# Sliding-window attention and a spectral mixing layer on one core: when the weights are prefetched, and into which slots

## The chip, the cores and the metric

The kernel runs on one core of a Trainium2 chip. The metric is the device time of one execution in microseconds (us). Ten runs of the kernel before took 462.46 to 473.84 us, with a median of 468.85 us.

The core has TensorE (PE, matmuls; PEld is its weight load), VectorE (DVE), ScalarE (ACT), GpSimd (POOL) and SyncE (SP). Here SP issues the plain DMA transfers, and POOL issues those that cast from fp32 to bf16 on the way. In the profile, q1 is SP's queue and q0 is POOL's.

## What is computed

The inputs are q, k and v of shape (8, 8, 576, 64) (batch, heads, sequence, head size), 64 pairs of weight matrices `w_r[m]`, `w_i[m]` of 512 x 512, and one matrix `w_ch` of 512 x 512, all fp32.

```python
# attention: window of 128 keys, a slope per head
scores = q @ k.T / sqrt(64) - slope[h] * |i - j|      # only 0 <= i - j < 128
x = softmax(scores) @ v                               # heads side by side: (8, 576, 512)

# spectral mixing
X = rfft(x, axis=1)                                   # the first 64 modes are used
Yr[b, m] = Xr[b, m] @ w_r[m] - Xi[b, m] @ w_i[m]
Yi[b, m] = Xr[b, m] @ w_i[m] + Xi[b, m] @ w_r[m]
u = x + irfft(Y, n=576, axis=1)                       # the other modes are zero
out = u + relu(u @ w_ch)                              # (8, 576, 512) fp32
```

Nearly all of the bytes are the 128 weight matrices. Each is 1 MB (1024 KB), and is used once, for all eight batches together.

## The kernel before, in words

**Attention.** The work is cut into 16 units. A unit is one batch element and four heads. A software pipeline runs over stages, and `STAGE` lists what is done in a stage, in the order in which each engine gets it, with a lag: an entry with lag -2 works on the unit that is two ahead. DVE casts the loaded fp32 q, k and v to bf16 (`cast`, L225), PE transposes q and k, ACT or DVE copies the result out of PSUM, PE makes the scores, ACT takes exp, DVE multiplies by a mask or PE adds a bias, PE multiplies by v, and DVE normalises into `x` (`norm`, L347). After every second unit the batch element is complete, and PE makes its 64 modes by a matmul with the table `F`; they are stored in `XC`.

The raw q, k and v lie in two slots each. `cast` of unit u ends with `load` of unit u + 2 into the slot that it has just read, so a load is issued only when DVE gets to that cast. Casts of q run three stages ahead, of k two ahead and of v in the unit's own stage. The last k load is therefore issued in stage 11, and the last v load in stage 13.

**The setup.** `_forward_table` (L71) makes `F` by a Sin on ACT, and then POOL puts the last rows of the table in place (L100 to L102). `distances` (L141) makes on POOL the two tables `near`, from which the masks (`decay`, ACT) and the biases (`offset`, DVE) of the heads are made. `fixtures` (L128) sets constant parts of the two v buffers and of the two `att` buffers on POOL. The masks and biases of heads 4 to 7 are made beside the first stages, from the list `side`.

**Weight tiles.** A weight tile is one matrix, numbered 0 to 127 in the order of use, `w_r[0]`, `w_i[0]`, `w_r[1]` and so on. `load_w` (L440) loads the next tiles in one of two forms. As bf16 a tile takes half the space and is issued by POOL. As fp32 it is issued by SP, and PE reads the upper halves of its numbers as bf16. Before the change tiles are loaded strictly in the order of use:

- In the attention, as bf16, into the pool `early` of `EARLY` = 14 slots: `AHEAD` gives for each stage how many. From stage 1 on a small copy (`gate`) makes POOL wait for the first `norm` of the stage before it issues them. `LATER` does the same for seven slots in the raw q, k and v buffers that are no longer needed (`spare`). Tiles 0 to 20 are loaded in this way.
- At the end of the attention, as fp32, into `NWA` = 6 slots that lie where attention buffers were: tiles 21 to 26.
- In the mixing, `AGAIN` = 12 bf16 tiles into the slots of `early` that come free (27 to 38), each issued after one of the first 12 tiles has been used; and from then on, fp32 tiles, each into the fp32 slot of the tile just used. When tile `K1` - 1 = 38 has been used, `NWB` = 2 more fp32 slots are opened, and the space is taken for `wch`, `Zs` and `XW`.

**Mixing.** For each tile PE runs four matmuls (L604). Four modes share a PSUM tile (`acc`), which DVE scales and PE transposes into `YT`. From tile `K1` on, PE also makes the product of `x` with `w_ch` between the weight matmuls (`project`, L574). After the last tile the inverse transform, relu and sum run over 36 output tiles, which SP stores.

**What sets the order.** Each engine has its instructions in program order (`manual_schedule`); there is no planner. POOL's queue holds the setup, the gates and all bf16 loads; SP's holds the q, k and v loads, then all fp32 loads, then the stores. An instruction that waits holds up all behind it in its queue.

Of the kernel before, what the change touches and what calls it, by code (L numbers as in the profile page):

```python
# [10 lines left out]
BF16 = mybir.dt.bfloat16  # L11
# [8 lines left out]
P = 128  # L20
# [6 lines left out]
FULL = 4  # L27
# [43 lines left out]
def _forward_table(nc, pool, F, S):  # L71


    NM = F.shape[2] // 2
    tok = pool.tile([P, FULL + 1], I32)
    nc.gpsimd.iota(tok[:, :FULL], [[P, FULL]], base=0, channel_multiplier=1)
    for bb in range(2):
        nc.gpsimd.iota(
            tok[64 * bb : 64 * bb + 64, FULL : FULL + 1], [[0, 1]],
            base=FULL * P, channel_multiplier=1,  # L80
        )
    mode = pool.tile([P, NM], I32)
    nc.gpsimd.iota(mode, [[1, NM]], base=0, channel_multiplier=0)
    prod = pool.tile([P, FULL + 1, NM], FP32)
    nc.vector.tensor_tensor(
        out=prod,
        in0=tok.unsqueeze(-1).broadcast_to([P, FULL + 1, NM]),
        in1=mode.unsqueeze(1).broadcast_to([P, FULL + 1, NM]),
        op=ALU.mult,
    )  # L90
    turn = pool.tile([P, FULL + 1, 2, NM], FP32)
    for ri in range(2):
        nc.vector.tensor_scalar(turn[:, :, ri, :], prod, float(S) / (4 - 2 * ri), 1.0 / S,
                                op0=ALU.add, op1=ALU.mult)
    whole = pool.tile([P, FULL + 1, 2, NM], FP32)
    nc.vector.tensor_scalar(whole, turn, MAGIC, MAGIC, op0=ALU.add, op1=ALU.subtract)
    nc.vector.tensor_tensor(out=turn, in0=turn, in1=whole, op=ALU.subtract)
    nc.scalar.activation(F[:, : FULL + 1].rearrange("p a b -> p (a b)"),
                         turn.rearrange("p a b c -> p (a b c)"), AF.Sin, scale=TWO_PI)
    nc.gpsimd.memset(F[:64, FULL + 1], 0.0)  # L100
    nc.gpsimd.tensor_copy(F[64:, FULL + 1], F[64:, FULL])
    nc.gpsimd.memset(F[64:, FULL], 0.0)  # L102


class _Attention:
# [19 lines left out]
        self.att = [fix.tile([P, FULL * 8 * P + 64], BF16, name=f"att{i}") for i in range(2)]  # L125
        self.loaded, self.casted, self.open = {}, {}, {}

    def fixtures(self):  # L128
        nc = self.nc
        for t, tail in zip(self.vb, self.vt):  # L130
            for half in range(2):
                row = slice(64 * half, 64 * half + 64)
                c0 = W * half
                nc.gpsimd.memset(t[row, :, :, :, W - c0 : 2 * W - c0], 0.0)
                nc.gpsimd.memset(t[row, :, :, :, c0 + D : c0 + W], 1.0)
            nc.gpsimd.memset(tail, 0.0)
            nc.gpsimd.memset(tail[64:96, :, :, D:], 1.0)
        for t in self.att:
            nc.gpsimd.memset(t[:, FULL * 8 * P :], 1.0)

    def distances(self, pool):  # L141

# [254 lines left out]
def kernel(  # L397
# [10 lines left out]
    nc = tc.nc  # L408
    ctx.enter_context(tc.manual_schedule(engines=ALL | {SP}))
    B, H, S, _ = q.shape  # L410
    NM, DM, _ = moe_w_r.shape
    AHEAD = {0: 1, 1: 1, 3: 1, 4: 1, 5: 1, 7: 1, 8: 1, 10: 1, 11: 1, 12: 2, 13: 2, 14: 1}
    EARLY, NWA, NWB, AGAIN = 14, 6, 2, 12
    LATER = {11: 1, 12: 2, 13: 1, 14: 1, 15: 2}
    HM = NM // 2

    const = ctx.enter_context(tc.tile_pool(name="const", bufs=1))
# [3 lines left out]
    F = const.tile([P, FULL + 2, 2 * NM], BF16, name="F")  # L421
# [5 lines left out]
    early = actx1.enter_context(  # L427
        tc.tile_pool(name="w1", bufs=EARLY, side="right", reuse_waits="tile")
    )
# [4 lines left out]
    vflat = raw["v"].rearrange("p u s h d -> p (u s h d)")  # L434
    spare += [vflat[:, 2 * DM * i :] for i in range(3)]
    spare = [t[:, : 2 * DM].bitcast(BF16).rearrange("p (a e) -> p a e", a=4) for t in spare]
    wq, homes = [], []

    def load_w(n, pool, bf16):


        for i in range(len(wq), min(len(wq) + n, 2 * NM)):
            src = (moe_w_r, moe_w_i)[i % 2][i // 2].rearrange("(p a) e -> p a e", a=4)
            homes.append(pool)
            if bf16:
                t = spare.pop(0) if pool is None else pool.tile([P, 4, DM], BF16, tag="w", name="w")
                nc.gpsimd.dma_start(out=t, in_=src)
                wq.append([t[:, a] for a in range(4)])
            else:
                t = pool.tile([P, 4, DM], FP32, tag="w", name="w")  # L450
                nc.sync.dma_start(out=t, in_=src)
                wq.append([t[:, a].bitcast(BF16)[:, 1::2] for a in range(4)])

    with ExitStack() as actx:
        at = _Attention(tc, actx, q, k, v, (ident, F, FT), x, XC, raw)
        n = len(at.units)
        for w, u in (("q", 0), ("k", 0), ("q", 1), ("k", 1), ("v", 0), ("v", 1)):
            at.load(w, u)
        done = set()

        def run(name, arg, u):
            if 0 <= u < n and (name, arg, u) not in done:
                done.add((name, arg, u))
                getattr(at, name)(u, arg)

        make_identity(nc, ident)
        pool = _Scratch(x[:, B - 2 :].rearrange("p b t c -> p (b t c)").bitcast(FP32))
        wt = at.ps.tile([P, P], FP32, tag="av", bufs=1, name="warm")
        for _ in range(24):
            nc.tensor.matmul(wt, lhsT=ident, rhs=ident, start=True, stop=True)  # L470
        _forward_table(nc, pool, F, S)
        nc.vector.memset(norm, 2.0 / S)
        nc.vector.memset(norm[:32], 1.0 / S)
        for t in at.qkT:
            nc.vector.memset(t[:, 1, :, S:], 0.0)
        at.distances(pool)
        at.fixtures()
        nc.gpsimd.memset(XC[:, 4 * NC * NM :], 0.0)
        run("cast", "q", 0)
        run("transpose", "q", 0)  # L480
        run("cast", "k", 0)
        run("transpose", "k", 0)
        run("evacuate", "q", 0)
        for h in (1, 3):
            at.decay(h)
        run("evacuate", "k", 0)
        run("score", 1, 0)
        for h in (1, 3, 0, 2):
            at.offset(h)
        run("cast", "q", 1)  # L490
        run("transpose", "q", 1)
        run("evacuate", "q", 1)
        run("score", 0, 0)
        run("exp", 1, 0)
        for h in (0, 2):
            at.decay(h)
        run("exp", 0, 0)
        run("cast", "k", 1)
        run("cast", "v", 0)
        side = {0: [(at.offset, 4), (at.offset, 5), (at.offset, 6), (at.offset, 7), (at.decay, 5),  # L500
                    (at.decay, 7)], 1: [(at.decay, 4), (at.decay, 6)]}
        lags = [lag for _, _, lag in STAGE]
        for stage in range(min(lags), n + max(lags)):
            for name, arg, lag in STAGE:
                run(name, arg, stage - lag)
                if name in ("transpose", "exp") and side.get(stage):
                    fn, h = side[stage].pop(0)
                    fn(h)
            for fn, h in side.pop(stage, ()):
                fn(h)  # L510
            if stage == 3:
                at.inverse_table()
            if stage in AHEAD:
                if stage:
                    b, g = at.units[stage - 1]
                    nc.gpsimd.tensor_copy(gate[:1, :1], x[:1, b, 0, 256 * g : 256 * g + 1])  # L516
                load_w(AHEAD[stage], early, True)
            if stage in LATER:
                load_w(LATER[stage], None, True)

    with ExitStack() as mctx:
        fix = mctx.enter_context(tc.tile_pool(name="fix", bufs=1))
        YT = fix.tile([P, 2, 4, B, 2, HM], BF16, name="YT")
        pool = mctx.enter_context(tc.tile_pool(name="fin", bufs=2))
        wpool = mctx.enter_context(tc.tile_pool(name="w", bufs=NWA, reuse_waits="tile"))
        load_w(NWA, wpool, False)
        pctx = ExitStack()
        ps = pctx.enter_context(tc.tile_pool(name="fps", bufs=2, space=PSUM))
# [60 lines left out]
        def warm():  # L589
            wt = ps.tile([P, DM], FP32, tag="warm", bufs=1, name="warm")  # L590
            for _ in range(6):
                nc.tensor.matmul(wt, lhsT=ident, rhs=wch[:, 0], start=True, stop=True)  # L592

        quads, side, todo = [], [], 0
        Zs = XW = wch = w2 = None
        K1 = EARLY + sum(LATER.values()) + NWA + AGAIN
        for g in range(NM // 4):
            acc = ps.tile([P, DM], FP32, tag="acc", bufs=2, name="acc")
            for i in range(8):
# [10 lines left out]
                    )  # L610
                k = 8 * g + i
                if k < AGAIN:
                    load_w(1, early, True)
                elif homes[k] not in (early, None):
                    load_w(1, homes[k], False)
                if k == K1 - 1:
                    actx1.close()
# [19 lines left out]
                elif 8 * g + i >= 2 * NM - 5:  # L637
                    if 8 * g + i < 2 * NM - 1:
                        warm()
                if k >= K1 and k % 2 == 0 and todo < len(tiles):  # L640
                    side.append(project(todo))
# [110 lines left out]
```

## Time and profile before

| | |
|---|---|
| runs, median | 468.85 us |
| profiled execution, time | 470.03 us |
| profiled execution, span | 468.3 us |
| PE, DVE, ACT, POOL busy | 341.1, 181.3, 159.0, 58.3 us |
| read from and written to HBM | 163.58 MB, 9.44 MB |
| first weight matmul of the mixing | 148.66 us |

The profile is of one execution. Its page cuts the span into 40 slices of 11.7 us; a digit is the busy share in tenths. The GB/s count the bytes as they land, so that a tile cast to bf16 counts half of what is read. The DMA share of a stretch adds the times of packets, which overlap a little, over 16 engines: full use shows as slightly over 1. A wait is listed as the engine and line that waited, what released it, and then microseconds in total, number of times, and the longest.

### The profile page before, as it was taken

Reading aid. Unit: us, or ns where it says so; the run is one execution under the profiler, and the core shown is the slowest. Engines: PE = TensorE matmul, PEld = TensorE weight load, DVE = VectorE, ACT = ScalarE, POOL = GpSimd, SP = SyncE. Lnnn points to the kernel's source line nnn. Section 1 sums busy time; section 2 is a strip of 40 time slices with the busy share of each in tenths; the row PEclk is TensorE's granted clock in tenths of the full one; section 3 lists DMA queues with packets and bytes.
Section 4 is the critical chain, followed back from the end, with each engine's and each line's share of the span. In section 5 each row is a group of like instructions: output and inputs, shape, how many; then the busy total and the mean of one; then the engine's idle time right before and its main releaser. Section 6 shows DMA issues by size and latency. Waiting matters only on the chain.

```text
span 468.3 us, 7360 instructions
## 1 busy us (share of the span) xinstructions
PE 341.1 (73%) x2975; PEld 188.3 (40%) x3006; DVE 181.3 (39%) x353; ACT 159.0 (34%) x211; POOL 58.3 (12%) x101
## 2 busy tenths in 40 slices
PE   3579899997296844347997767876778687598994
PEld 3357667675265511113433333333333233233331
DVE  5879699993473200001211202121111120104785
ACT  4779799997081000000111111111102011003773
POOL 5600001021121201000000000000000000000654
PEclk8679899999699966557999999899989899869998
DMA  8899999999899999997999999999999999980787
GB/s 284 252 303 336 304 264 304 308 302 232 187 205 319 328 316 316 315 297 212 422 423 421 418 423 422 418 421 421 418 423 421 419 422 421 421 371 33 242 285 250
DMA packets 52146, 155.67 MB, mean 332 GB/s; under 512 B 3984, under 2 KB 22928, under 8 KB 39952
## 3 DMA queue, kind: packets, MB, share of 16 engines
q1 hardware_dynamic: 46832, 137.38, 77.1%
q0 software_dynamic: 5280, 17.83, 19.3%
q8 instruction: 23, 0.38, 0.3%
q14 instruction: 11, 0.09, 0.1%
HBM read 163.58 MB, written 9.44 MB: 369 GB/s over the span
## 4 chain that ended last, share of the span: by engine, by line
DMA 56%; PE 20%; DVE 10%; issue 7%; ACT 4%; POOL 2%; POOLq 0%; DVEq 0%; ACTq 0%
DMA w<-in_moe_w_r_dram 40%; DMA w<-in_moe_w_i_dram 8%; PE acc L604 7%; DMA kr<-in_k_dram 5%; PE av L331 3%; DVE x L347 2%; DMA qr<-in_q_dram 2%; PE warm L592 1%; DVE vb L233 1%; DVE att L305 1%; PE tp L250 1%; ACT r L686 1%; PE my L585 1%; DVE k L238 1%; DVE o L695 1%
## 5 line engine op out<-in xcount | busy, mean ns | idle before, releaser
L604 PE MATMUL acc<-w,XC 128*32 128x512 bf16 x484 | 133.6, 430 | 69.5 <-DMA w<-in_moe_w_i_dram 34.4
L604 PEld LDWEIGHTS <-XC 128*32 128x32 bf16 x512 | 59.8, 138 | 128.2 <-issue 99.2
L587 ACT CAST XW<-my 128x512 bf16<-128x512 f32 x36 | 21.1, 586 | 219.5 <-PE my L585 143.7
L294 ACT ACTIVATE att<-sc 128x1024 bf16<-128x1024 f32 x64 | 64.2, 1031 | 9.8 <-PE sc L284 9.8
L581 DVE COPY xT<-tr 128x512 bf16<-128x512 bf16 x36 | 15.3, 425 | 116.9 <-PE tr L579 116.9
L689 POOL TENSOR_TENSOR r<-r,x 128x512 f32<-128x512 f32 x18 | 20.8, 1158 | 261.5 <-ACT r L686 261.5
L331 PE MATMUL av<-vb,att 128*128 128x132 bf16 (+1 forms) x576 | 40.3, 223 | 17.2 <-DVE x L347 15.4
L331 PEld LDWEIGHTS <-att 128*128 128x128 bf16 x704 | 38.6, 101 | 23.1 <-issue 9.9
L585 PE MATMUL my<-wch,xT 128*128 128x512 bf16 x134 | 38.1, 394 | 7.9 <-DVE xT L581 7.3
L533 DVE TENSOR_SCALAR yq<-acc 128x512 bf16<-128x512 f32 x15 | 10.3, 686 | 73.6 <-PE acc L604 73.6
L256 ACT COPY qkT<-tp 128x1152 bf16<-128x1152 bf16 x30 | 33.5, 1115 | 13.9 <-PE tp L250 13.3
L284 PE MATMUL sc<-qkT 64*64 64x256 bf16 (+2 forms) x640 | 26.2, 272 | 7.8 <-ACT qkT L256 3.9
L347 DVE TENSOR_TENSOR x<-av,rec 128x640 bf16<-128x640 f32 x32 | 26.4, 825 | 1.1
L695 DVE TENSOR_TENSOR o<-yy,r 128x512 f32<-128x512 f32 x36 | 23.7, 688 | 6.5 <-ACT r L686 4.9
L233 DVE CAST vb<-vr 64x1024 bf16<-64x1024 f32 x32 | 22.8, 711 | 6.5 <-DMA vr<-in_v_dram 6.3
L686 ACT ACTIVATE r<-mm 128x512 f32<-128x512 f32 x36 | 21.2, 597 | 9.0 <-PE mm L676 5.0
L284 PEld LDWEIGHTS <-qkT 64*64 64x64 bf16 x640 | 14.9, 111 | 22.0 <-issue 16.4
L585 PEld LDWEIGHTS <-xT 128*128 128x128 bf16 x144 | 11.4, 100 | 28.9 <-issue 11.3
L564 ACT CAST Zs<-zw 64x512 bf16<-64x512 f32 x16 | 9.2, 578 | 34.9 <-PE zw L555 34.7
L305 DVE TENSOR_TENSOR att<-att,mask 128x1024 bf16<-128x1024 bf16 x32 | 20.6, 684 | 0.0
L565 DVE CAST Zs<-z 64x512 bf16<-64x512 f32 x16 | 11.0, 688 | 18.1 <-PE z L558 18.0
L516 POOL COPY gate<-x 1x1 bf16<-1x1 bf16 x11 | 5.4, 490 | 97.9 <-DVE x L347 97.9
(93 smaller groups left out, 336.1 us busy)
## 6 DMA issues: line engine op xcount, KB each, us to landing
w<-in_moe_w_i_dram SPq DMA_DIRECT2D x48, 1024.0 KB, 18.8
w<-in_moe_w_r_dram SPq DMA_DIRECT2D x47, 1024.0 KB, 18.8
qr<-in_q_dram SPq DMA_DIRECT2D x16, 576.0 KB, 8.4
kr<-in_k_dram SPq DMA_DIRECT2D x16, 576.0 KB, 7.8
vr<-in_v_dram SPq DMA_DIRECT2D x32, 256.0 KB, 7.5
out_dram<-o SPq DMA_DIRECT2D x32, 256.0 KB, 2.5
w<-in_moe_w_r_dram POOLq DMA_DIRECT2D x13, 512.0 KB, 9.4
w<-in_moe_w_i_dram POOLq DMA_DIRECT2D x13, 512.0 KB, 9.5
```

The source lines that it names most:

```text
L233: nc.vector.tensor_copy(self.vb[u % 2][row, :, :, :, W * half : W * half + D], src[row, :2])
L256: (self.nc.vector.tensor_copy if u < 2 and w == "q" else self.nc.scalar.copy)(dst.rearrange("q h (p j) -> q h p j", j=TPP), tp.rearrange(" ...
L284: nc.tensor.matmul(sc[64 * half : 64 * half + 64, e, j * 256 + c0 : j * 256 + c0 + n], lhsT=qkT[row, 1, h, k0 + j : k0 + P : 2], rhs=qkT[r ...
L294: self.nc.scalar.activation(self.att[u % 2][:, kt * 8 * P : (kt + 1) * 8 * P], sc.rearrange("p e n -> p (e n)"), AF.Exp, scale=1.0 / math. ...
L305: nc.vector.tensor_tensor(out=rows, in0=rows, in1=self.table[:, heads], op=ALU.mult)
L331: nc.tensor.matmul(bank[:, qt * W : qt * W + rhs[j].shape[1]], lhsT=att[:, o : o + P], rhs=rhs[j], start=(n == 0 and j == 0), stop=(n == l ...
L347: nc.vector.tensor_tensor(out=self.x[:, b, :, cs].rearrange("p t (h d) -> p h t d", h=2), in0=tiles[:, :, :, :D], in1=rec.unsqueeze(-1).br ...
L585: nc.tensor.matmul(mm, lhsT=xT[:, dt], rhs=wch[:, dt], start=(dt == 0), stop=(dt == 3))
L587: nc.scalar.copy(XW[:, i], mm)
L604: nc.tensor.matmul(acc[32 * (i // 2) : 32 * (i // 2) + 32], lhsT=XC[:, c0 : c0 + 31 * NM + 1 : NM], rhs=w[a], start=(ri == 0 and a == 0), ...
L686: nc.scalar.activation(r, mm, AF.Relu)
L695: nc.vector.tensor_tensor(out=o, in0=yy, in1=r, op=ALU.add)
```

## The change

The diff changes five things.

1. `_forward_table` becomes a generator: it stops after the Sin, and POOL's last steps on `F` run between the first and the second half of the fixtures, after `distances`.
2. The biases of the first heads are made in the order 0, 2, 1, 3, and the eight side steps for heads 4 to 7 all run in stage 0, two of them at each transpose.
3. The prefetch: one tile moves from stage 3 to stage 2. The tiles of stage 12 (two in `early` and two spare) and one spare tile of stage 11 are dropped from there. Stage 13 loads four, stage 14 four, stage 15 three: 20 tiles instead of 21.
4. The transition: `load_w` can take a chosen tile, and the tiles not yet loaded are kept in a list. The eight recycled bf16 slots get tiles 24, 26, ... 38, and the fp32 slots get the numbers between in order (20 to 23, 25, 27, 29, ...).
5. `AGAIN` is 8 instead of 12; `K1` is computed from the last chosen tile and is 39 as before.

```diff
@@ _forward_table @@
     nc.scalar.activation(F[:, : FULL + 1].rearrange("p a b -> p (a b)"),
                          turn.rearrange("p a b c -> p (a b c)"), AF.Sin, scale=TWO_PI)
+    yield
     nc.gpsimd.memset(F[:64, FULL + 1], 0.0)
     nc.gpsimd.tensor_copy(F[64:, FULL + 1], F[64:, FULL])
     nc.gpsimd.memset(F[64:, FULL], 0.0)
@@ fixtures @@
-    def fixtures(self):
+    def fixtures(self, i):
         nc = self.nc
-        for t, tail in zip(self.vb, self.vt):
+        for t, tail in ((self.vb[i], self.vt[i]),):
...
-        for t in self.att:
-            nc.gpsimd.memset(t[:, FULL * 8 * P :], 1.0)
+        nc.gpsimd.memset(self.att[i][:, FULL * 8 * P :], 1.0)
@@ the kernel's function @@
-    AHEAD = {0: 1, 1: 1, 3: 1, 4: 1, 5: 1, 7: 1, 8: 1, 10: 1, 11: 1, 12: 2, 13: 2, 14: 1}
-    EARLY, NWA, NWB, AGAIN = 14, 6, 2, 12
-    LATER = {11: 1, 12: 2, 13: 1, 14: 1, 15: 2}
+    AHEAD = {0: 1, 1: 1, 2: 1, 4: 1, 5: 1, 7: 1, 8: 1, 10: 1, 11: 1, 13: 4, 14: 1}
+    LATER = {14: 3, 15: 3}
+    EARLY, NWA, NWB, AGAIN = 14, 6, 2, 8
...
-    wq, homes = [], []
+    wq, homes, todo_w, again = {}, {}, list(range(2 * NM)), []

-    def load_w(n, pool, bf16):
+    def load_w(n, pool, bf16, chosen=None):
-        for i in range(len(wq), min(len(wq) + n, 2 * NM)):
+        for i in ([i for i in todo_w if i not in again][:n] if chosen is None else chosen):
+            todo_w.remove(i)
             src = (moe_w_r, moe_w_i)[i % 2][i // 2].rearrange("(p a) e -> p a e", a=4)
-            homes.append(pool)
+            homes[i] = pool
...
-        _forward_table(nc, pool, F, S)
+        table = _forward_table(nc, pool, F, S)
+        next(table)
...
         at.distances(pool)
-        at.fixtures()
+        at.fixtures(0)
+        next(table, None)
+        at.fixtures(1)
...
-        for h in (1, 3, 0, 2):
+        for h in (0, 2, 1, 3):
             at.offset(h)
...
-        side = {0: [(at.offset, 4), (at.offset, 5), (at.offset, 6), (at.offset, 7), (at.decay, 5),
-                    (at.decay, 7)], 1: [(at.decay, 4), (at.decay, 6)]}
+        side = {0: [(at.offset, 4), (at.offset, 6), (at.decay, 5), (at.offset, 5), (at.decay, 7),
+                    (at.offset, 7), (at.decay, 4), (at.decay, 6)]}
...
                 if name in ("transpose", "exp") and side.get(stage):
-                    fn, h = side[stage].pop(0)
-                    fn(h)
-            for fn, h in side.pop(stage, ()):
-                fn(h)
+                    for _ in range(1 + (name == "transpose")):
+                        fn, h = side[stage].pop(0)
+                        fn(h)
...
         wpool = mctx.enter_context(tc.tile_pool(name="w", bufs=NWA, reuse_waits="tile"))
+        first = todo_w[0]
+        again = [first + 4 + 2 * i for i in range(AGAIN)]
         load_w(NWA, wpool, False)
...
-        K1 = EARLY + sum(LATER.values()) + NWA + AGAIN
+        K1 = again[-1] + 1
...
                 if k < AGAIN:
-                    load_w(1, early, True)
+                    load_w(1, early, True, again[k : k + 1])
```

More of the change, by code (lines that the diff above doesn't have):

```diff
@@ L447, in load_w @@
                 nc.gpsimd.dma_start(out=t, in_=src)
-                wq.append([t[:, a] for a in range(4)])
+                wq[i] = [t[:, a] for a in range(4)]
             else:
@@ L451, in load_w @@
                 nc.sync.dma_start(out=t, in_=src)
-                wq.append([t[:, a].bitcast(BF16)[:, 1::2] for a in range(4)])
+                wq[i] = [t[:, a].bitcast(BF16)[:, 1::2] for a in range(4)]
     with ExitStack() as actx:
```

## The prediction

> **What bounds the kernel now.** I read the page first: its slices over time and its DMA queues.
>
> ```profile
> span 468.3 us, 7360 instructions
> ...
> DMA  8899999999899999997999999999999999980787
> GB/s 284 252 303 336 304 264 304 308 302 232 187 205 319 328 316 316 315 297 212 422 423 421 418 423 422 418 421 421 418 423 421 419 422 421 421 371 33 242 285 250
> ...
> q1 hardware_dynamic: 46832, 137.38, 77.1%
> q0 software_dynamic: 5280, 17.83, 19.3%
> ...
> DMA 56%; PE 20%; DVE 10%; issue 7%; ACT 4%; POOL 2%; POOLq 0%; DVEq 0%; ACTq 0%
> ```
>
> The DMA engines are busy in nearly every slice up to 420 us. The low GB/s before slice 19 are partly a matter of counting: a tile that is cast to bf16 on the way is read as 1 MB and counted as the 0.5 MB that land. So 315 GB/s with half of the tiles cast is 315 x 4/3 = 420 GB/s read, the same rate as the 422 later. The DMA is therefore the bound until the last weight lands, whatever the engines do, and what can be saved is the time in which the DMA engines have nothing to do. The second view is the table of stretches, which shows where that is (stretch, its length, PE, PEld, DVE, ACT and POOL busy, clock, DMA share, GB/s). The share counts overlapping packets, so a saturated stretch shows 1.01 to 1.07.
>
> ```profile
> 2.00:16.00 14.00, 5.71 (x63) 4.11 (x61) 9.68 (x18) 6.25 (x9) 9.63 (x22) 0.70 1.07 337
> 16.00:20.00 4.00, 2.75 (x40) 1.41 (x37) 3.99 (x5) 3.31 (x4) 3.83 (x8) 0.77 0.61 200
> 20.00:100.00 80.00, 69.30 (x1250) 54.54 (x1262) 70.80 (x129) 70.84 (x81) 7.28 (x16) 0.94 1.07 299
> ...
> 112.00:124.00 12.00, 4.22 (x76) 3.39 (x75) 1.85 (x4) 3.88 (x6) 0.00 (x0) 0.84 1.07 236
> 124.00:130.00 6.00, 3.94 (x45) 3.38 (x44) 4.63 (x9) 0.74 (x1) 2.04 (x4) 0.50 0.65 124
> ...
> 200.00:212.00 12.00, 5.59 (x12) 1.55 (x12) 0.00 (x0) 0.00 (x0) 0.00 (x0) 0.50 1.05 286
> 212.00:218.50 6.50, 4.70 (x21) 1.89 (x21) 1.31 (x5) 0.00 (x0) 0.00 (x0) 0.70 0.47 88
> 218.50:418.00 199.50, 151.74 (x689) 67.14 (x701) 32.24 (x80) 25.74 (x44) 0.00 (x0) 0.95 1.01 421
> ```
>
> Three holes stand out: 16 to 20 us, 124 to 130 us and 212 to 218.5 us. Each is priced as its length times one minus its share over its neighbours' share: 4 x (1 - 0.61/1.07) = 1.7 us; 6 x (1 - 0.65/1.07) = 2.3 us; 6.5 x (1 - 0.47/1.05) = 3.6 us. Together 7.6 us. In 112 to 124 the engines stand still (DVE busy 1.85 of 12 us) and yet the DMA is full. Who is late there is told by the waits from 108 to 128 us (us in total, times, longest), and the third hole by SP's own waits:
>
> ```profile
> DVE vb L233 <- DMA vr<-in_v_dram: 6.3, 1, 6.3
> DVE k L238 <- DMA kr<-in_k_dram: 2.9, 1, 2.9
> DVE q L238 <- DMA qr<-in_q_dram: 2.0, 1, 2.0
> DVE vt L235 <- DMA vr<-in_v_dram: 1.2, 1, 1.2
> ```
>
> ```profile
> SPq L451 <- PE acc L604: 98.0, 43, 34.3
> ```
>
> The attention loses 6.3 + 2.9 + 2.0 + 1.2 = 12.4 us to its own last loads, and in the third hole SP has waited 34.3 us for PE to free an fp32 slot.
>
> **What the Trainium skill says.** "DMA: Bandwidth & Descriptors", section "Queues, rings and completion order": an engine takes turns between the queues that have work, a packet at a time. The trace agrees, and shows what that means for unequal packets. From 105 to 120 us the POOL queue q0 had 706 packets and SP's queue q1 807, nearly one to one, but q0 held 85.2% of the engines' time and q1 20.0%, because a weight row is 8 KB read and a v row 512 bytes. A k load (issued at 100.11) took 24.1 us to land. The same page, "Issuing engines are not separate DMA queues": work issued by SP and by POOL shares the same 16 engines. It agrees: with both queues running from 148 to 200 us the share is 1.04, not more. "HBM Reference", section "Access", gives about 425 GB/s for a core streaming alone; here it is 421 from 218.5 to 418 us. One 1.0486 MB tile thus costs 1.0486/0.421 = 2.49 us of DMA, and moving it in time gains nothing by itself.
>
> **The setup.** POOL waits 3.61 us for the Sin at L101, and L100 to L102 stand from 1.88 to 6.83 us, ahead of the distances. With these behind the first half of the fixtures the distances end 4.9 us sooner. Waiting on them are the bias at L176 (DVE idle 2.66 us) and the mask at L173 (ACT idle 2.31 us). Then DVE goes on right after its copy that ends at 7.95 us, and the casts after that, each of which issues the load of two units later, come up to 2.66 us sooner. So do the loads missing in the first hole. POOL's wait of 3.61 us vanishes, and its first weight load (19.37 us) comes about 3.6 us sooner, into the same hole; q, k and v loads beside it are held up as they were by it before. After 20 us the DMA is full again, so a longer lead of the compute gains nothing: the most is the 1.7 us of the hole. The least is 0; I take 1.3. The order of the biases and of the side decays (eight pieces, all in stage 0 now) moves DVE pieces of 0.66 us and ACT pieces of 0.6 us within stretches where the DMA is full: nothing; if that cover went, up to 1.3 us for two decays, two pieces of 0.6, counted in the lower end.
>
> **The weight of stage 3 in stage 2.** One load goes from 43.37 us to about 35 us. The DMA is full on both sides: 0. If it makes a q, k or v load late, the engines wait up to 2.5 us, but the DMA works on meanwhile.
>
> **The prefetch held back.** Before, POOL issues six tiles between 100.35 and 110.36 us; after, one, and nothing in stage 12. Five tiles leave the stretch: 5 x 2.49 = 12.4 us of DMA. The attention should regain about its 12.4 us, but the five tiles have to be loaded later: the two cancel. What counts is idle DMA. The hole at 124 to 130 us is there because stage 13 and its gate were late; it goes: -2.3 us. Against it, the DMA may now run dry before the held-back tiles start. Counting the trace's packets by size, 3.2 MB were asked for and not yet read at 100.35 us (about 2.1 loads of q or k, one of v, 1.3 weights). At some 385 GB/s, what I count as read from 100 to 110 us, that lasts 8.3 us, to 108.7. v of unit 14, asked for at about 105 us, adds 0.59 MB, 1.75 us at 340 GB/s: to 110.4. Unit 13's v cast (before at 118.32 after its wait) would then stand at about 110.4 to 112.2, and frees the slot for the last v load; POOL's gate opens after the next norm, two to three DVE pieces on, at about 113.6. Between 110.4 and 112.2 the DMA is idle, from then on the last v load fills it. New idle: 1.8 us; at 421 GB/s throughout it would be 3 us, with slower draining 0. Behind the gate on POOL stand only further weight loads, and who waits for these is PE, after the attention. From 113.6 us eleven bf16 tiles are 27 us of DMA; the first six fp32 loads, which wait for attention memory (139.99 to 146.7 us before), come some 12 us sooner, so no hole opens at the end of the attention.
>
> **Every second tile recycled.** Now the twelve bf16 tiles are one block, numbers 27 to 38, and 39 to 46 load at the same time into eight fp32 slots. The two queues go half and half, so all arrive near 212 us; PE waits for 38, then has to free slots before SP can issue (216.33 us). After, the eight bf16 tiles are every second number from 24 to 38, and the fp32 tiles the numbers between: what arrives together is used together, each tile used frees a slot, and SP never sits on a full pool. While q0 has tiles, it covers any short gap of q1; when it ends, q1 has up to eight slots out. The hole goes: -3.6 us; by bytes not read it is up to 4.4 us, and 0 if q1 restarts as late as now. PE has room: four matmuls take 1.05 us per tile against 2.49 us. Five more tiles come in fp32 instead of bf16: both are read at 420 GB/s, 0.
>
> **Sum.** -1.3 - 2.3 + 1.8 - 3.6 = -5.4 us. What follows the last weight (420 to 468.3 us) is unchanged. The profiled execution took 470.03 us, 1.7 us more than its span, so 464.6 for it; it lies 1.2 us above the median of 468.85, so for the median 463.4 us.
>
> **The rivals.** (1) The DMA conserves more than I think: the dry spell before the gate is 5 us, and the third hole only goes by half. -1.3 - 2.3 + 5 - 1.8 = -0.4, about 468.4 us. For it: only two v loads are asked for after 100.4 us. Against: 3.2 MB of backlog. (2) The holes are worth more: counted by bytes, the second is 3.2 us and the third 4.4, and the queue doesn't run dry: -1.7 - 3.2 - 4.4 = -9.3, 459.5 us. (3) Slower: the gate of stage 13 opens late. It waits for a norm that stands on DVE behind the cast of the last k, and that load competes with two weights. Each microsecond that the gate is later than 113.6 is a microsecond of idle DMA once the last v has landed. From about 119 us on the gain is used up; at 124 us, close to the 126.14 of today, it is 10.4 us more: +5.0, 473.9 us. Against: q1 has the engines nearly alone, and the median k load took 7.8 us.
>
> **The numbers.** Forecast 0.50, rival (1) 0.23, rival (2) 0.15, rival (3) 0.12. The range of 458.5 to 469.0 reaches from the end of rival (2) to the end of rival (1), and leaves out most of rival (3) and the tails. About 1% (4.7 us) is what a measurement of this kernel can tell from no change. Over 1% faster: most of the forecast, and rival (2), 0.57; within 1%: rival (1) and the forecast's weak end, 0.32; over 1% slower: rival (3), 0.11.
>
> **What would show it.** The setup: no wait of DVE at L176, and a DMA share above 0.9 from 16 to 20 us. The prefetch: no DVE wait over 2 us for vr or kr, the first recycled tiles used some 12 us sooner, and at most 2 to 3 us of low share between 105 and 115 us. The transition: no SP wait near 34 us, and 420 GB/s read through 218 us. The last weight then lands near 414 us, with some 48 us after it. I am wrong if the dry spell is longer, or if the end of the kernel isn't set by the last weight.

## The result, and the profile after

The changed kernel takes 460.79 us (median of 15 runs, 459.83 to 463.28), the kernel before 468.18 us (median of 52, 462.46 to 473.84). The ratio is 0.9887, with a 95% interval of 0.9862 to 0.9912: 1.1% faster, or 5.3 us of 468.18 (4.1 to 6.5). It compares only the runs near each kernel's fastest, and the kernel before scatters more, so it lies nearer to 1 than the quotient of the medians, 0.984 (7.4 us). Kernels that ran on different chips are compared by their medians below. The forecast was 463.4 us, 5.4 us less than the median given. The total was right; two of the terms that make it were not, as the experiments show. What is said above of the DMA share, "full use shows as slightly over 1", doesn't hold the other way round: a share over 1 doesn't show that the DMA sets the pace.

The profiled execution of the changed kernel took 460.68 us, with a span of 458.9 us, against 470.03 and 468.3 before. The two profiles are 9.4 us apart, more than the medians, since the one of before is of an execution 1.9 us above its median. First the page of the changed kernel: the span, the DMA over 40 slices, the two queues and the chain.

```profile
span 458.9 us, 7358 instructions
...
DMA  8999999997999999999999999999999999971677
GB/s 284 324 338 310 308 309 295 332 291 178 219 316 315 280 317 317 350 406 421 422 421 419 421 422 420 422 418 422 418 423 422 419 422 421 420 328 68 230 275 252
...
q1 hardware_dynamic: 47552, 142.62, 80.8%
q0 software_dynamic: 4560, 15.21, 16.6%
...
DMA 58%; PE 17%; DVE 12%; issue 5%; ACT 4%; POOL 1%; POOLq 0%; ACTq 0%; DVEq 0%
```

The slice with 212 GB/s (the nineteenth of before) is gone; a dip has come in the tenth slice (178). Five tiles have moved from q0 to q1. The stretches say the same with lengths; the last two columns are DMA share and GB/s.

```profile
16.00:20.00 4.00, 3.03 (x33) 1.71 (x34) 3.97 (x8) 3.62 (x6) 2.46 (x5) 1.00 1.07 360
20.00:100.00 80.00, 72.14 (x1331) 56.59 (x1331) 72.20 (x130) 72.42 (x80) 8.06 (x16) 1.00 1.09 310
104.00:112.00 8.00, 7.48 (x142) 5.88 (x140) 6.74 (x14) 7.55 (x10) 2.57 (x5) 1.00 0.61 152
112.00:124.00 12.00, 10.34 (x187) 7.92 (x189) 9.21 (x19) 10.07 (x12) 4.57 (x8) 1.00 1.06 213
124.00:130.00 6.00, 3.71 (x68) 3.37 (x68) 3.00 (x6) 0.39 (x2) 0.00 (x0) 1.00 1.04 292
...
212.00:218.50 6.50, 4.59 (x24) 2.28 (x24) 1.64 (x6) 1.17 (x2) 0.00 (x0) 1.00 1.01 422
```

All three holes of before are closed: 16 to 20 us now has a share of 1.07, 124 to 130 us 1.04, 212 to 218.5 us 1.01. A new one stands at 104 to 112 us. By the same arithmetic as in the prediction it is 8 x (1 - 0.61/1.06) = 3.4 us. Two stretches of 2 us within it:

```profile
106.00:108.00 2.00, 1.85 (x38) 1.54 (x36) 1.93 (x5) 1.93 (x4) 0.00 (x0) 1.00 0.24 57
110.00:112.00 2.00, 1.98 (x43) 1.61 (x40) 1.01 (x3) 1.70 (x3) 1.38 (x3) 1.00 0.68 117
```

And a row of the longer table that should have been the same is not: 20 to 100 us has 310 GB/s instead of 299, and DVE is busy 72.20 us in it instead of 70.80.

The gates of POOL mark the stages. In order of time (start, length, what, idle before it), those of stages 1, 2, 4, 5 and 11, and of stage 13:

```profile
25.29 0.18 POOL L519 COPY gate<-x 1x1 bf16<-1x1 bf16 x1 [6.71 <-DVE x L347]
33.40 0.58 POOL L519 COPY gate<-x 1x1 bf16<-1x1 bf16 x1 [7.44 <-DVE x L347]
48.24 0.57 POOL L519 COPY gate<-x 1x1 bf16<-1x1 bf16 x1 [13.80 <-DVE x L347]
55.33 0.57 POOL L519 COPY gate<-x 1x1 bf16<-1x1 bf16 x1 [6.04 <-DVE x L347]
...
95.11 0.57 POOL L519 COPY gate<-x 1x1 bf16<-1x1 bf16 x1 [5.22 <-DVE x L347]
108.81 0.51 POOL L519 COPY gate<-x 1x1 bf16<-1x1 bf16 x1 [12.65 <-DVE x L347]
```

Before, stages 1, 5 and 11 opened at 27.94, 60.06 and 99.84 us. The lead is 2.65 us at the first gate and 4.7 us at the other two; the second experiment shows that some 2 us of the 4.7 are scatter. The first weight matmul starts at 130.92 us instead of 148.66. No wait of DVE for vr or kr is left between 90 and 130 us. The last weight matmul begins at 414.29 us instead of 424.00, so 43 to 44 us remain after its end in both: the tail is the same.

Two theories go into the experiments. Theory A is the prediction's: the DMA is full between 20 and 100 us, so that only holes can be won. Theory B: the attention is paced by its engines, a share over 1 is packets in flight and not a bound, and a lead of the engines reaches the last weight. The times below are medians. Kernels of one section shared a chip unless the text says otherwise; the changed kernel itself is taken from its own runs, beside a kernel before at 468.18 us.

### The profile page after: what moved, and what is told of

It reads as the page before. It is cut to its first block, busy times and chain, and to the rows that moved or that the text cites. A ratio compares the mean times of both kernels' runs of the same rounds, so it can differ in the third digit from the quotient of the medians.

```text
span 458.9 us, 7358 instructions
## 1 busy us (share of the span) xinstructions
PE 343.0 (75%) x2975; PEld 189.6 (41%) x3006; DVE 180.9 (39%) x353; ACT 159.6 (35%) x211; POOL 57.9 (13%) x95
## 4 chain that ended last, share of the span: by engine, by line
DMA 58%; PE 17%; DVE 12%; issue 5%; ACT 4%; POOL 1%; POOLq 0%; ACTq 0%; DVEq 0%
DMA w<-in_moe_w_i_dram 41%; DMA wch<-in_moe_w_ch_dram 9%; DMA w<-in_moe_w_r_dram 8%; PE acc L609 4%; PE av L331 3%; DVE vb L233 2%; DVE x L347 2%; DVE att L305 2%; PE tp L250 2%; DVE q L238 2%; DVE k L238 1%; PE warm L597 1%; ACT r L691 1%; PE mm L681 1%; PE xt L368 1%
## 5 line engine op out<-in xcount | busy, mean ns | idle before, releaser
L609 PE MATMUL acc<-w,XC 128*32 128x512 bf16 x488 | 131.7, 419 | 67.4 <-DMA w<-in_moe_w_r_dram 37.5
L609 PEld LDWEIGHTS <-XC 128*32 128x32 bf16 x512 | 61.8, 137 | 135.2 <-issue 105.4
L331 PE MATMUL av<-vb,att 128*128 128x132 bf16 (+1 forms) x576 | 38.4, 217 | 3.9 <-DVE x L347 2.1
L331 PEld LDWEIGHTS <-att 128*128 128x128 bf16 x704 | 36.5, 98 | 9.5 <-DVE x L347 6.4
L700 DVE TENSOR_TENSOR o<-yy,r 128x512 f32<-128x512 f32 x36 | 23.6, 688 | 6.9 <-ACT r L691 4.8
L590 PEld LDWEIGHTS <-xT 128*128 128x128 bf16 x144 | 11.4, 99 | 28.1 <-issue 10.2
L569 ACT CAST Zs<-zw 64x512 bf16<-64x512 f32 x16 | 9.2, 578 | 34.4 <-PE zw L560 34.3
L271 PE MATMUL sc<-bias,ident 128*128 128x512 bf16 x48 | 17.0, 410 | 1.6 <-ACT att L294 1.6
```

The source lines that it names most:

```text
L331: nc.tensor.matmul(bank[:, qt * W : qt * W + rhs[j].shape[1]], lhsT=att[:, o : o + P], rhs=rhs[j], start=(n == 0 and j == 0), stop=(n == l ...
L590: nc.tensor.matmul(mm, lhsT=xT[:, dt], rhs=wch[:, dt], start=(dt == 0), stop=(dt == 3))
L609: nc.tensor.matmul(acc[32 * (i // 2) : 32 * (i // 2) + 32], lhsT=XC[:, c0 : c0 + 31 * NM + 1 : NM], rhs=w[a], start=(ri == 0 and a == 0), ...
L700: nc.vector.tensor_tensor(out=o, in0=yy, in1=r, op=ALU.add)
```

## One part at a time

Four kernels on one chip, each with one part of the change, beside the kernel before (468.35 us there).

**The setup alone** (all of points 1 and 2 of the change):

```diff
                          turn.rearrange("p a b c -> p (a b c)"), AF.Sin, scale=TWO_PI)
+    yield
...
+        at.fixtures(0)
+        next(table, None)
+        at.fixtures(1)
...
-        for h in (1, 3, 0, 2):
+        for h in (0, 2, 1, 3):
...
+        side = {0: [(at.offset, 4), (at.offset, 6), (at.decay, 5), (at.offset, 5), (at.decay, 7),
+                    (at.offset, 7), (at.decay, 4), (at.decay, 6)]}
...
```

> The kernel before with the setup parts of the change alone (POOL's last steps on F behind the first half of the fixtures, order of biases and side pieces); prefetch and transition as before. Theory A (the prediction: DMA is full from 20 to 100 us, so only the hole at 16 to 20 us can be won): 1.3 us faster, at most 1.7. Theory B (the attention is paced by its engines and the DMA has slack that the share hides, so every microsecond of lead counts): the lead of 2.7 us at the first gate stays and reaches the last weight, 2.5 to 5 us faster.

Measured: 464.38 us, ratio 0.9911 (0.9870 to 0.9952), 4.2 us faster (2.2 to 6.1). Theory A's most, 1.7 us, lies outside the interval. But the ten runs spread over 9.1 us, and in the profiled one, the fastest, the hole behind the attention's stall is nearly gone too (lowest share of 4 us 0.94), so a part of the 4.2 us may be the stall's. The kernel with the setup undone, below, has no stall. The wait that the change of the setup removes is this one of the kernel before (from 0 to 20 us); it is gone in the changed kernel:

```profile
DVE bias L176 <- POOL x L155: 2.7, 1, 2.7
```

The gates (starts of stages 1, 3, 4, 5) show the lead of the changed kernel, without any other part of it:

```profile
25.09 0.18 POOL L518 COPY gate<-x 1x1 bf16<-1x1 bf16 x1 [6.71 <-DVE x L347]
39.48 0.57 POOL L518 COPY gate<-x 1x1 bf16<-1x1 bf16 x1 [13.73 <-DVE x L347]
48.06 0.57 POOL L518 COPY gate<-x 1x1 bf16<-1x1 bf16 x1 [7.53 <-DVE x L347]
55.14 0.57 POOL L518 COPY gate<-x 1x1 bf16<-1x1 bf16 x1 [6.04 <-DVE x L347]
```

**The prefetch held back, alone:**

```diff
-    AHEAD = {0: 1, 1: 1, 3: 1, 4: 1, 5: 1, 7: 1, 8: 1, 10: 1, 11: 1, 12: 2, 13: 2, 14: 1}
-    EARLY, NWA, NWB, AGAIN = 14, 6, 2, 12
-    LATER = {11: 1, 12: 2, 13: 1, 14: 1, 15: 2}
+    AHEAD = {0: 1, 1: 1, 3: 1, 4: 1, 5: 1, 7: 1, 8: 1, 10: 1, 11: 1, 13: 4, 14: 1}
+    EARLY, NWA, NWB, AGAIN = 14, 6, 2, 13
+    LATER = {14: 3, 15: 3}
```

> The kernel before with the prefetch of stages 11 to 15 alone held back (no tile in stage 12, four in stage 13, four in 14, three in 15, one bf16 tile less in the attention and one more recycled, 13 instead of 12), the tile of stage 3 left there, setup and order of the tiles as before. Theory A (the prediction): 2.3 us of idle DMA go and 1.8 come, 0.5 us faster. Theory B (counting the bytes of the two traces): the dry spell costs 3.2 to 3.4 us and the hole at 124 to 130 us gives back 2.4, up to 1 us slower. Both: the engines' 12.4 us of waits for the last q, k and v go and the attention ends some 12 us sooner, with next to nothing of it in the time.

Measured: 466.51 us, ratio 0.9984 (0.9960 to 1.0008): no change that can be told from none (the medians are 1.8 us apart). The mixing starts at 134.46 us instead of 148.66, and nothing of these 14 us is in the time. The dry spell (here 106 to 116 us, share 0.78: 10 x (1 - 0.78/1.07) = 2.7 us) costs about what the hole behind the stall had cost, 2.3 us.

```profile
106.00:116.00 10.00, 8.87 (x169) 7.13 (x166) 8.73 (x17) 8.89 (x11) 2.57 (x5) 1.00 0.78 199
```

This trace also tells how much of the lead is the setup's. As far as the gate of stage 11 this program is the kernel before. Its gate of stage 1 opens at 27.82 us, as there (27.94), but that of stage 5 1.9 us sooner; first this kernel's, then that of before:

```profile
58.19 0.57 POOL L516 COPY gate<-x 1x1 bf16<-1x1 bf16 x1 [6.04 <-DVE x L347]
60.06 0.57 POOL L516 COPY gate<-x 1x1 bf16<-1x1 bf16 x1 [6.44 <-DVE x L347]
```

The granted clock of PE from 50 to 60 us was 1.00 here and 0.90 there. So 1.9 of the 4.7 us of lead are scatter between executions. Against this trace the changed kernel leads by 2.5 us in stage 1 and 2.9 us in stages 5 and 11, about the 2.66 us of DVE's wait at L176, kept through the attention.

**The transition alone:**

```diff
-    EARLY, NWA, NWB, AGAIN = 14, 6, 2, 12
+    EARLY, NWA, NWB, AGAIN = 14, 6, 2, 8
...
+        first = todo_w[0]
+        again = [first + 4 + 2 * i for i in range(AGAIN)]
...
-                    load_w(1, early, True)
+                    load_w(1, early, True, again[k : k + 1])
```

> The kernel before with the transition alone changed: after the 21 tiles of the attention the recycled bf16 slots get every second tile (25, 27 to 39), eight instead of twelve, and the fp32 slots the tiles between; setup and prefetch as before. Theory A: the hole at 212 to 218.5 us goes, 3.6 us faster. Theory B: the same place, counted in bytes 4.4 us. If the hole only moves, 0.

Measured: 465.52 us, ratio 0.9941 (0.9911 to 0.9971), 2.8 us faster (1.4 to 4.2). The hole at the transition is gone (212 to 218.5 us). The hole behind the attention's stall is still there, at another time and deeper in this execution:

```profile
132.00:136.00 4.00, 0.59 (x6) 0.60 (x7) 3.40 (x7) 0.00 (x0) 0.52 (x2) 0.50 0.12 35
136.00:140.00 4.00, 3.73 (x61) 3.22 (x59) 2.90 (x6) 1.81 (x2) 1.00 (x2) 0.72 0.74 113
212.00:218.50 6.50, 5.94 (x27) 2.61 (x27) 0.85 (x2) 1.17 (x2) 0.00 (x0) 0.90 1.02 427
```

Priced against 1.07, 132 to 140 us lose 4 x (1 - 0.12/1.07) + 4 x (1 - 0.74/1.07) = 4.8 us, where the kernel before lost 2.3 in its profile; DVE had waited up to 10.9 us for one v load.

**The tile of stage 3 in stage 2, alone:**

```diff
-    AHEAD = {0: 1, 1: 1, 3: 1, 4: 1, 5: 1, 7: 1, 8: 1, 10: 1, 11: 1, 12: 2, 13: 2, 14: 1}
+    AHEAD = {0: 1, 1: 1, 2: 1, 4: 1, 5: 1, 7: 1, 8: 1, 10: 1, 11: 1, 12: 2, 13: 2, 14: 1}
```

> The kernel before with the one bf16 tile of stage 3 loaded in stage 2, nothing else. Theory A: 0. Theory B: the lead of the changed kernel grew from 2.7 us at the first gate to 4.7 us at the fifth stage; if this move makes it, 1.5 to 2 us faster, and if the setup makes it (through PE's clock, which the setup leaves at half from 8 to 28 us before), 0 here and the larger lead in the run with the setup alone.

Measured: 468.46 us, 0.1 us above the kernel before; ratio 0.9967 (0.9940 to 0.9994). The two disagree, and no step in the trace stands behind a gain: the gate of stage 5 opens at 60.41 us, no sooner than before (60.06). The lead is not from here. Nor does the setup of before leave PE's clock at half: from 8 to 28 us the granted clock is 0.59 in the profile of before, but 1.00 in this kernel, with the same setup.

By the medians the parts are worth 4.0, 1.8, 2.8 and -0.1 us alone, 8.5 us in all, and 7.4 together: they don't simply add up.

## Is the DMA a bound in the attention?

**The setup undone** in the changed kernel, so that prefetch and transition stay:

```diff
-        table = _forward_table(nc, pool, F, S)
-        next(table)
+        _forward_table(nc, pool, F, S)
...
-        at.fixtures(0)
-        next(table, None)
-        at.fixtures(1)
+        at.fixtures()
...
-        for h in (0, 2, 1, 3):
+        for h in (1, 3, 0, 2):
...
```

> The changed kernel (median 460.79 us) with the setup parts undone. Theory A (a lead of the compute is worth only the hole at 16 to 20 us): about 462.1 us, 1.3 slower than the changed kernel. Theory B (the attention is paced by its engines, so the lead counts in full): 464.5 to 465.5 us, some 4 slower, and the gates of POOL 2.7 us later from stage 1 on and up to 4.7 later from stage 5 on.

Measured: 464.32 us (462.02 to 466.30), 3.5 us above the changed kernel (459.83 to 463.28). They ran on two chips, with the kernel before at 468.19 and 468.18 us. The gates of stages 1 and 5 open 2.6 and 4.15 us later than in the changed kernel; the second figure holds scatter, as shown above:

```profile
27.90 0.18 POOL L517 COPY gate<-x 1x1 bf16<-1x1 bf16 x1 [7.84 <-DVE x L347]
59.48 0.57 POOL L517 COPY gate<-x 1x1 bf16<-1x1 bf16 x1 [7.05 <-DVE x L347]
```

This is close to theory B's 464.5 to 465.5 us, and well above theory A's 462.1.

**A delay in the middle of the attention.** The changed kernel, with DVE held up after stage 6 by work that nothing needs:

```diff
+    idle = const.tile([P, 448], FP32, name="idle")
...
+        nc.vector.memset(idle, 1.0)
...
+            if stage == 6:
+                for _ in range(5):
+                    nc.vector.tensor_tensor(out=idle, in0=idle, in1=idle, op=ALU.mult)
```

> The changed kernel with five extra operations of DVE (448 fp32 elements each on a tile that nothing reads, some 0.6 us each, 3 us in all) after stage 6, in the middle of the attention. Theory A (the DMA is full there and sets the pace): nothing, 460.8 us. Theory B (the engines set the pace; a share over 1 is packets waiting, not a bound): the 3 us come in full, 463.5 to 464 us, and the gates after stage 6 are 3 us later.

Measured: 464.96 us (463.65 to 466.52), 4.2 us above the changed kernel, again with the kernel before at 468.19 us (ratio 0.9927, 0.9894 to 0.9960). The five operations took 3.25 us together (65.81 to 69.06 us). The memset that fills their tile takes 0.43 us of DVE in the setup, and the gate of stage 1 opens at 25.30 us all the same (25.29 in the changed kernel). The gates of stages 5, 7, 8 and 10 are:

```profile
56.40 0.58 POOL L524 COPY gate<-x 1x1 bf16<-1x1 bf16 x1 [6.58 <-DVE x L347]
72.60 0.57 POOL L524 COPY gate<-x 1x1 bf16<-1x1 bf16 x1 [15.15 <-DVE x L347]
79.31 0.57 POOL L524 COPY gate<-x 1x1 bf16<-1x1 bf16 x1 [5.67 <-DVE x L347]
93.06 0.57 POOL L524 COPY gate<-x 1x1 bf16<-1x1 bf16 x1 [12.43 <-DVE x L347]
```

At stage 5, ahead of the delay, this execution is 1.1 us late already (56.40 against 55.33); at stages 7 and 10 it is 4.2 us late (3.8 at stage 8). So some 3 us of the delay come through, and theory A's nothing is refuted. A q, k or v load waits for DVE's cast to free one of two slots, so the DMA can't run further ahead of DVE than that: a later cast is a later load. From 66 to 76 us the DMA share fell to 0.83. The time is 1 us above theory B's 463.5 to 464 us; why is not shown.

**A tile in every stage.** Theory B in its strong form says that there is room for more weights in the attention. One tile in each of the stages 0 to 13:

```diff
-    AHEAD = {0: 1, 1: 1, 2: 1, 4: 1, 5: 1, 7: 1, 8: 1, 10: 1, 11: 1, 13: 4, 14: 1}
+    AHEAD = {**{i: 1 for i in range(14)}, 14: 0}
```

> The changed kernel with one bf16 tile in each of the stages 0 to 13: tiles 3, 6, 9 and 12 of the list come in the stages 3, 6, 9 and 12, and stage 13 loads one instead of four, stage 14 three; 20 tiles in all as in the changed kernel. Theory A (the DMA is full in the attention, a tile moved into it takes its 2.49 us from the q, k and v loads): no faster than with the tile in stage 12 alone (458.8 us), and slower by up to 7 us where the attention is then paced by its loads. Theory B (the DMA has slack that the share hides): three tiles more are 7.5 us of DMA; what of them fits into slack comes off the end, 455 to 457.5 us.

And one tile more in stage 6, with one in stage 12 and two in stage 13:

```diff
-    AHEAD = {0: 1, 1: 1, 2: 1, 4: 1, 5: 1, 7: 1, 8: 1, 10: 1, 11: 1, 13: 4, 14: 1}
+    AHEAD = {0: 1, 1: 1, 2: 1, 4: 1, 5: 1, 6: 1, 7: 1, 8: 1, 10: 1, 11: 1, 12: 1, 13: 2, 14: 1}
```

> The changed kernel with one bf16 tile more in stage 6 and one in stage 12, two in stage 13: one tile moved into the middle of the attention. Theory A: 458.8 us, as with the one in stage 12 alone. Theory B: the slack of a stage without a weight is about 1.5 us (6.7 us of stage less 5.2 us for q, k and v at 340 GB/s), 457 to 457.8 us.

Measured: 461.0 us with a tile in every stage and 460.12 us with one in stage 6, neither faster than one tile in stage 12 alone (458.8 us, next section). They ran on another chip than that one, with the kernel before at 467.17 us there; the ratios to it are 0.9887 (0.9844 to 0.9930) and 0.9862 (0.9829 to 0.9894). So what the strong form of theory B expected, 455 to 457.8 us, didn't come. Two things stand in the trace of the kernel with a tile in every stage: DVE's waits from 20 to 130 us, and a stretch late in the attention.

```profile
DVE q L238 <- DMA qr<-in_q_dram: 7.9, 6, 2.0
```

```profile
120.00:124.00 4.00, 3.67 (x65) 2.49 (x64) 2.75 (x6) 3.52 (x4) 2.88 (x6) 1.00 0.28 31
```

First, the engines now wait for q loads: 7.9 us in six places, against 1.4 us in one in the changed kernel, and the mixing starts at 137.14 us instead of 130.92. Second, the DMA runs dry near the end. The gate of stage 13 opens at 115.02 us, 6.2 us later, and one tile is left behind it where the changed kernel has four. From 112 to 124 us the share is 0.88 for 8 us and 0.28 for 4: priced as before, 8 x (1 - 0.88/1.06) + 4 x (1 - 0.28/1.06) = 4.3 us, more than the dry spell of the changed kernel. The second kernel has both as well, by less (4.3 us of waits for q; a share of 0.94 from 112 to 124 us). So the two runs show that the engines set the pace only by little, as 2.5 us of DMA more in a stage already make them wait; they don't show what a tile there is worth with stage 13 left full.

## What the dry spell costs

**One tile, and two, in stage 12** of the changed kernel, instead of in stage 13:

```diff
-    AHEAD = {0: 1, 1: 1, 2: 1, 4: 1, 5: 1, 7: 1, 8: 1, 10: 1, 11: 1, 13: 4, 14: 1}
+    AHEAD = {0: 1, 1: 1, 2: 1, 4: 1, 5: 1, 7: 1, 8: 1, 10: 1, 11: 1, 12: 1, 13: 3, 14: 1}
```

> The changed kernel with one of the four bf16 tiles of stage 13 loaded in stage 12 instead. It is work for the dry spell of 3.2 us between 104 and 112 us, one tile is 2.49 us of DMA. Theory 1 (the dry spell costs its length): 2 to 2.5 us faster than the changed kernel, 458.3 to 458.8 us, with no wait for v. Theory 2 (its 8 KB packets hold up the last v loads, and the stall comes back): the same or slower than 460.8 us.

In the second kernel stage 12 loads two and stage 13 two.

> The changed kernel with two of the four bf16 tiles of stage 13 in stage 12, as in the kernel before (which had two more in the raw slots there). 5 us of DMA for a dry spell of 3.2. Theory 1: the spell is gone and a part of the last loads is late by 1 to 2 us, 457.6 to 458.8 us. Theory 2 (waits behind 8 KB packets): DVE waits for vr or kr return, 3 us or more, and it is no faster than with one tile.

Measured: 458.8 us (458.09 to 460.62), ratio 0.9792 (0.9748 to 0.9836), and 458.59 us (456.95 to 459.62), ratio 0.9777 (0.9734 to 0.9820). By the medians both beat the changed kernel, by 2.0 and 2.2 us, on two chips with the kernel before at 468.19 and 468.18 us. In the kernel with one tile the stretch that was dry is full:

```profile
104.00:112.00 8.00, 7.39 (x141) 5.90 (x139) 6.77 (x13) 7.60 (x9) 2.04 (x4) 1.00 1.01 231
```

No wait of DVE for vr or kr comes back in either. The second tile adds nothing that can be told. So the stall of before isn't made by weights in stage 12 as such. More likely it is their number: six tiles were issued there within 10 us in stages 11 and 12, where these kernels issue two and three. At which number it sets in was not tried, nor whether it matters that three of the six went into raw slots.

## Which part of the setup

Two more kernels, on two chips, made from the changed kernel: one keeps POOL's part of the setup alone (order of biases and side pieces as before; its diff is shown), the other the order alone (POOL's part as before).

```diff
-        for h in (0, 2, 1, 3):
+        for h in (1, 3, 0, 2):
...
-        side = {0: [(at.offset, 4), (at.offset, 6), (at.decay, 5), (at.offset, 5), (at.decay, 7),
-                    (at.offset, 7), (at.decay, 4), (at.decay, 6)]}
+        side = {0: [(at.offset, 4), (at.offset, 5), (at.offset, 6), (at.offset, 7), (at.decay, 5),
+                    (at.decay, 7)], 1: [(at.decay, 4), (at.decay, 6)]}
...
```

> The changed kernel with the order of the first biases and of the side pieces as before, so that of the setup only POOL's part stays (the last steps on F behind the first half of the fixtures). If the wait of DVE for the distances (2.7 us) makes the lead: 460.8 us, as the changed kernel. If the order of the side pieces makes the 1.5 us more that the lead grows between stages 2 and 5: about 462.3 us, with the first gate as early as in the changed kernel and the gate of stage 5 some 1.5 us later.

> The changed kernel with POOL's part of the setup undone, and the order of the first biases and of the side pieces as changed. With no setup part the median was 464.32 us, with POOL's part alone 462.0, with both 460.79. If the order is worth its 1.2 us by itself: about 463.1 us. If it is worth nothing by itself, and the 1.2 us were the scatter of PE's clock: about 464.3 us. If it delays something while POOL is late: over 464.8 us.

Measured: 462.0 us with POOL's part alone, 464.63 us with the order alone, against 464.32 with neither and 460.79 with both. By these medians POOL's part takes off 2.3 us, close to the 2.66 us that DVE had waited for the distances; the four ran on four chips, where the kernel before had 467.17, 468.42, 468.19 and 468.18 us, so a microsecond of it is uncertain. The order by itself does nothing that can be told (464.63), and its gate of stage 5 opens at 58.35 us, as in the kernel with the prefetch held back, which has no part of the setup (58.19).

On top of POOL's part the order looks like 1.2 us, again between chips. With POOL's part alone the gate of stage 5 opens at 56.53 us, 1.2 us later than in the changed kernel, but two kernels with the new order have it as late (56.40 with the delay, which comes after that gate, and 56.51 with two tiles in stage 12). In all three the granted clock of PE from 40 to 50 us is 0.83, and it is 1.00 in the changed kernel. So this microsecond of the gate goes with the clock and not with the order; whether the 1.2 us in the time are the clock too stays open.

## Why the prediction was right in total, and where it was not

- **The bound after the attention: right.** Holes in the DMA from 130 us on decide. 14 us of earlier mixing in the kernel with the prefetch held back left the time where it was, and the tail after the last weight matmul is 43 to 44 us in both kernels. The prediction's figure of about 425 GB/s stands in the Trainium skill's "HBM Reference", section "Specifications (TRN2)"; the trace of before has 421.
- **The transition, -3.6 us: right.** The hole is closed in every kernel with alternating tiles, and the part alone measured 2.8 us (1.4 to 4.2). One step of it went otherwise: SP does still sit on a full pool, once for 23.6 us (34.3 before), but the DMA share is 1.04 to 1.05 from 132 to 160 us meanwhile, with POOL's tiles in flight.
- **The setup, -1.3 us: wrong.** The step that failed is "After 20 us the DMA is full again, so a longer lead of the compute gains nothing: the most is the 1.7 us of the hole." It measured 4.2 us alone and 3.5 when undone. A share of 1.07 was read as a full DMA. In its place: a load waits for DVE's cast to free one of two slots, the engines set the pace, and DVE's 2.66 us at L176 go through the whole attention (2.5 to 2.9 us at the gates); by the medians POOL's part, which removes that wait, is worth 2.3 us of time. What the setup measured beyond these 2.7 us is not accounted for. The prediction named the wait and its size and then wrote it off. Two sizes on the way were off as well: the distances end 3.1 us sooner, not 4.9 (10.58 and 7.45 us), as POOL's steps at L155 to L166 take longer than before, and the first weight load is issued 1.6 us sooner, not 3.6 (17.80 us).
- **The prefetch, -2.3 + 1.8 = -0.5 us: right in sum, mis-sized in both terms.** Alone it measured 0.75 us by the ratio, within an interval that holds 0. The dry spell is 3.4 us in the changed kernel, beyond the bound of 0 to 3 given; filling it won 2.0 us. The backlog and the time of the gate were about right (13.2 us from the tile of stage 11 to the gate, both predicted and measured). What the estimate seems to have left out is the start of a queue that has run empty: the last v load is issued from 106.59 us and the next weight at 109.25 us, yet the share is 0.24 from 106 to 108 us and 0.68 from 110 to 112 us. That is a reading of one trace; no run varied it. On the other side the hole behind the stall, 2.3 us in the profile of before, was 4.8 us in the profile of the transition alone.
- **The stage 2 tile and five more fp32 tiles, 0:** nothing was seen that contradicts it; the first was measured with medians 0.1 us apart and a ratio that just excludes 1.
- **The rivals.** Rival (1)'s dry spell of 5 us came in part, its half-closed third hole did not. Rival (2)'s 459.5 us is nearer to the median of 460.79 us than the forecast's 463.4, but not for its reason: a queue that doesn't run dry was a part of it. Rival (3), a late gate, did not come: the last k load was in time.

So 463.4 us came from a setup that was two to three microseconds too small and a dry spell 1.6 us too short. By the ratio 5.3 us were gained, by the medians 7.4; the forecast of 5.4 agrees with the first, but not for all of its reasons. That the two errors went against each other is luck.

## What to carry to other kernels

A busy share of the DMA near or over 1 doesn't say that the DMA sets the pace: ask who lets the next load go. Here that was a cast on a busy engine, and a delay of 3.25 us on that engine, in a stretch where the changed kernel has a share of 1.09, came out as 4.2 us at the end. The margin can be small: one tile more in each stage without one made the engines wait for loads. A short delay put into the middle of the stretch answers the question in one run. Before reading a lead from two traces, look at a third of the same program: here two executions of the same instructions were 1.9 us apart by stage 5. Where prefetch is held back from a critical load, weigh the work that is left against the time until the next tile is let go; here one tile left in that place was worth 2 us.

## What the runs showed that was not expected

- The kernel before scatters: over 11.4 us in 52 runs (462.46 to 473.84), where the changed one spreads over 3.5 in 15. The stall's hole differs between profiled executions: in the stretches of 4 us around it the lowest share is 0.58 before, 0.12 with the transition alone, 0.24 with the stage 2 tile alone, and 0.94 with the setup alone. On one chip the kernel with the prefetch held back, which has no stall, spread over 6.1 us in 22 runs and the one with the stage 2 tile alone, which has it, over 10.4 in 22. So the stall probably makes a part of the spread; no run isolates it.
- Weights on q0 can leave q1 little of the DMA: with the transition alone a single v load kept DVE waiting 10.9 us. From 116 to 128 us the two queues had 612 and 821 packets, and q0 held 92.3% of the engines' time, q1 14.4%.
